# Attention blocks and MoE 1 groups in another order, some vector work on other engines

## Chip, cores and metric

One core of one Trainium2 chip runs the whole program. The metric is the device time of one execution, in microseconds; lower is better.

## The reference

Attention over 4 batches, 8 heads, 576 positions, head size 64 (heads 0 to 3 with a local mask of 32 positions, heads 4 to 7 with a mask of equal position modulo 32), and behind it two feed-forward stages on 2304 tokens of 512 columns, all in float32:

```python
scores = np.where(masks[None], scale * np.matmul(q, k.transpose(0, 1, 3, 2)), -1e9)
attn = np.exp(scores - np.max(scores, axis=-1, keepdims=True))
attn = attn / (np.sum(attn, axis=-1, keepdims=True) + 1e-09)
x = np.matmul(attn, v).transpose(0, 2, 1, 3).reshape(B * S, H * D)
h = x @ w_in                                    # 512 -> 2048
x = (h * np.tanh(softplus(h))) @ w_out          # MoE 1 (Mish), 2048 -> 512
g = x @ w_gate
y = (g / (1 + np.exp(-g)) * (x @ w_val)) @ w_out2   # MoE 2 (SwiGLU), 512 -> 1536 -> 512
```

## The kernel before

**Precision.** Each float32 operand of a big matmul is kept as a high part and a low part (what is left). A product is three matmuls of 512 columns: high by high, high by low, low by high (`mm3`, L81 to L83). `split_hi` copies to the high part, on ScalarE (L74); `split_lo` subtracts (L79), on VectorE or GpSimd. The weights come as 64-bit numbers; each weight tile of 128 x 512 is turned into float32 by four steps (`w_ops`: a at L206 and L207, b L210, c L213, d L216), each one VectorE instruction, the first with a square on ScalarE besides; step d also issues the load of a later weight (`w_load`, L138). Then `w_hi` (ScalarE) and `w_lo` split it. `w_step(n)` does n of these steps, `w_flush` the splits.

**Attention.** There are 48 units (16 pairs of heads, 3 units each; unit 3i + 2 is the last of pair i). Two units make a block; `at_pair` issues block k by the list PAIR, whose entries are a function and a lag: it works on units 2k and 2k + 1 and finishes older ones, down to unit 2k - 5. The steps of a unit: `at_qk` (scores on TensorE, L303, and mask, minimum and copy on VectorE, L315), `at_exp` (ScalarE, L330), `at_norm` (1e-9 added on VectorE, L343, reciprocal on VectorE, L344, multiply on GpSimd, L345), `at_tr` (transposes on TensorE, L360), `at_copy` (VectorE, L374), `at_pv` (TensorE, L387), `at_hi` (ScalarE) and `at_lo` (VectorE) into `xh` and `xl`, the input of MoE 1. `at_load` and `at_v` issue the transfers of q, k and v on SP's queue. Blocks 0 to 23 start units; 24 to 26 only finish.

**MoE 1.** The work is in stages n = 0 to 19: n = 5q + c is column chunk q of the hidden layer and token chunk c. A stage's first half is 16 groups (`g1_step`: hidden tile f, input tile kc, one `mm3` each); after kc = 3 the result h is copied out by VectorE (`act_a` with keep, L489). Then `act_m` does the four Mish on ScalarE, with a table load ahead of and behind them (L495, L496), `act_c` splits the results into `g`, and the second half is 16 more groups (`g2_by_e`). Input tile kc of tokens 0 to 511 needs the low parts of unit 3kc + 2 of the first batch; the next chunk needs units 12 to 23.

**The order** is written out by hand; each engine runs its queue in that order. First ten dummy matmuls (`spin`, L733) and the first loads. Then a loop of 15 steps k: block k; dummies by KEEP (6 in steps 1 to 5); `w_flush` and WSTEPS[k] weight steps; up to two groups of FIRST, each with a due time; and entries of the list `todo` (Mish, splits of g). With 15 blocks done the rest of stages n = 1 and 2 and the second halves of n = 0 and 1 follow, 58 groups from the point where block 15 starts; behind each group `fill` is called, every fifth of which starts a block. From n = 3 on there is no attention left.

## Time and profile before

| | us |
|---|---|
| median of 3 runs (lowest, highest) | 918.61 (917.64, 918.65) |
| the profiled execution | 920.39 |
| its span | 918.60 |
| TensorE busy | 900.7 (98%) |
| VectorE busy | 597.4 (65%) |
| ScalarE busy | 384.3 (42%) |
| GpSimd busy | 157.2 (17%) |

PE is TensorE, PEld its weight loads, DVE is VectorE, ACT is ScalarE, POOL is GpSimd, SPq the queue that issues transfers. A row of the timeline is one instruction, or several alike (xcount), with its start, its duration, and in brackets the idle time ahead of it and what ended that. Matmuls overlap, so prices are read from start to start. PEclk is the granted clock of TensorE, 1.00 being full speed.

### The profile page before, as it was taken

To read this page: it belongs to the slowest core of one execution; us is meant where nothing else is said; L and a number is where in the kernel's file an instruction comes from. 1 tells how busy PE (TensorE), PEld (TensorE's weight loads), DVE (VectorE), ACT (ScalarE), POOL (GpSimd) and SP (SyncE) were. 2 spreads that over 40 slices of the span, in tenths; PEclk is the share of its full clock that TensorE was granted. 3 is DMA by queue.
4 is the path that set the end of the run, shared out by engine and by line. 5 is a ranking of instruction groups with operands and counts; after the bars stand their busy time and mean duration, and the time that the engine had idled before them with its cause. 6 is when DMAs were issued, how large, how long until landed. Compare 5 with 4: busy or idle time off the path is not lost.

```text
span 918.6 us, 13867 instructions
## 1 busy us (share of the span) xinstructions
PE 900.7 (98%) x4984; PEld 754.8 (82%) x4984; DVE 597.4 (65%) x1382; ACT 384.3 (42%) x951; POOL 157.2 (17%) x153
## 2 busy tenths in 40 slices
PE   8988999999999999999999999999999999999998
PEld 5776877888888888888889888888888888888886
DVE  4896656768977797769556788848435644334434
ACT  4767765525443444435233553423324423322230
POOL 1333331400000000000022322203113221112211
PEclk8979999999999999999999999999999999999999
DMA  7876431324653255424106888675532545552322
GB/s 266 297 242 213 144 100 39 131 93 150 213 180 121 92 184 185 165 85 161 70 1 250 302 328 303 260 286 189 189 118 112 207 152 192 185 204 86 144 92 92
DMA packets 48499, 156.70 MB, mean 171 GB/s; under 512 B 5296, under 2 KB 11824, under 8 KB 48432
## 3 DMA queue, kind: packets, MB, share of 16 engines
q1 hardware_dynamic: 48432, 155.83, 47.7%
q8 instruction: 39, 0.64, 0.3%
q14 instruction: 28, 0.23, 0.1%
HBM read 119.64 MB, written 36.18 MB: 170 GB/s over the span
## 4 chain that ended last, share of the span: by engine, by line
PE 93%; DVE 2%; ACT 1%; POOL 1%; DMA 1%; issue 1%; SPq 0%; ACTq 0%; POOLq 0%; DVEq 0%
PE y L83 21%; PE h L83 21%; PE o L83 16%; PE cXv L83 7%; PE cXg L83 7%; PE c L83 4%; PE cZv L83 4%; PE cZg L83 4%; PE sc L303 2%; PE xp L387 2%; PE cYv L83 2%; PE cYg L83 2%; PE tp L360 1%; PE wp L733 1%; DMA qk<-in_qk_dram 1%; ACT pt L330 1%
## 5 line engine op out<-in xcount | busy, mean ns | idle before, releaser
L83 PE MATMUL y<-g,w 128*128 128x512 f32 (+1 forms) x960 | 202.0, 369 | 0.0
L83 PEld LDWEIGHTS y<-g,w 128*128 128x128 f32 x960 | 167.0, 189 | 29.9
L83 PE MATMUL h<-xh,w 128*128 128x512 f32 (+1 forms) x640 | 190.9, 375 | 0.0
L83 PE MATMUL o<-wr,fs 128*128 128x512 f32 x648 | 149.6, 389 | 0.0
L83 PEld LDWEIGHTS o<-wr,fs 128*128 128x128 f32 x648 | 121.3, 188 | 25.0
L83 PEld LDWEIGHTS h<-xh,w 128*128 128x128 f32 x640 | 117.9, 191 | 20.4
L83 PE MATMUL h<-xl,w 128*128 128x512 f32 (+1 forms) x320 | 119.0, 372 | 0.0
L491 ACT ACTIVATE u<-h 128x512 f32<-128x512 f32 (+1 forms) x68 | 37.2, 547 | 140.7 <-PE h L83 140.7
L79 POOL TENSOR_TENSOR fs<-k,fs 128x512 fp32r<-128x512 f32 x36 | 48.5, 1346 | 267.5 <-ACT fs L74 206.4
L720 DVE TENSOR_TENSOR acc<-acc,o 128x512 f32<-128x512 f32 x90 | 61.3, 685 | 48.5 <-PE o L83 48.5
L330 ACT ACTIVATE pt<-pt,sm 108x64 f32<-108x64 f32 (+1 forms) x160 | 55.8, 351 | 35.2 <-DVE sm L315 34.0
L83 PEld LDWEIGHTS h<-xl,w 128*128 128x128 f32 x320 | 61.2, 191 | 9.7
L79 POOL TENSOR_TENSOR B<-acc,B 128x512 fp32r<-128x512 f32 x6 | 8.4, 1395 | 297.6 <-ACT B L74 297.6
L74 ACT CAST fs<-k 128x512 fp32r<-128x512 f32 x36 | 22.4, 622 | 87.9 <-DVE k L675 37.6
L83 PE MATMUL cXv<-T,wr 128*128 128x512 f32 x216 | 55.0, 390 | 0.0
L83 PE MATMUL cXg<-T,wr 128*128 128x512 f32 x216 | 54.9, 389 | 0.0
L661 DVE TENSOR_TENSOR k<-cZg,k 128x512 f32<-128x512 f32 x12 | 8.3, 692 | 71.1 <-PE cZg L83 71.1
L79 DVE TENSOR_TENSOR g<-u,g 128x512 fp32r<-128x512 f32 (+1 forms) x68 | 43.1, 654 | 13.9 <-ACT g L74 13.9
L74 ACT CAST ws<-wt 128x512 fp32r<-128x512 f32 x60 | 37.0, 616 | 36.0 <-DVE wt L216 29.1
L74 ACT CAST g<-u 128x512 fp32r<-128x512 f32 (+1 forms) x80 | 44.6, 574 | 15.8 <-PE y L83 15.7
L83 PEld LDWEIGHTS cXv<-T,wr 128*128 128x128 f32 x216 | 40.5, 188 | 8.7 <-ACT k L658 0.3
L83 PEld LDWEIGHTS cXg<-T,wr 128*128 128x128 f32 x216 | 40.5, 188 | 8.6 <-DVE k L661 0.2
(102 smaller groups left out, 1419.7 us busy)
## 6 DMA issues: line engine op xcount, KB each, us to landing
raw<-in_w_dram SPq DMA_DIRECT2D x54, 512.0 KB, 3.8
qk<-in_qk_dram SPq DMA_DIRECT2D x16, 898.0 KB, 6.7
wr<-wd_g_S SPq DMA_DIRECT2D x24, 512.0 KB, 6.7
wr<-wd_v_S SPq DMA_DIRECT2D x24, 512.0 KB, 7.4
wr<-wd_p SPq DMA_DIRECT2D x24, 512.0 KB, 4.6
wr<-wd_g_W SPq DMA_DIRECT2D x18, 512.0 KB, 6.3
wr<-wd_v_W SPq DMA_DIRECT2D x18, 512.0 KB, 7.1
rawl<-in_w_dram SPq DMA_DIRECT2D x14, 512.0 KB, 5.8
```

The source lines that it names most:

```text
L74: nc.scalar.copy(hi, src)
L79: eng.tensor_tensor(out=lo, in0=src, in1=hi.bitcast(F32), op=ALU.subtract)
L83: nc.tensor.matmul(o, lhsT=lhs, rhs=rhs, start=first and i == 0, stop=last and i == 2, skip_group_check=more)
L303: nc.tensor.matmul(sc[:2 * nq, jj * w:(jj + 1) * w], lhsT=t[:, 2 * j * nq:2 * (j + 1) * nq], rhs=t[:, QW + j0:QW + j0 + nk], start=True, s ...
L330: nc.scalar.activation(out=pt[:, jj], in_=pt[:, jj], func=AF.Exp, scale=-1.0, bias=sm[:, 0, jj:jj + 1], accum_out=sm[:, 1, jj:jj + 1],)
L360: nc.tensor.transpose(tp[:k, o:o + n], src, ident[:n, :n])
L387: nc.tensor.matmul(xp[64 * h:64 * h + 64, o:o + nq - skip], lhsT=vt[:nk, jj, 64 * h:64 * h + 64], rhs=ts[:nk, c0 + h * nq + skip:c0 + (h + ...
L491: nc.scalar.activation(out=u, in_=p, func=AF.Mish)
L661: nc.vector.tensor_tensor(out=t, in0=p, in1=t, op=ALU.add)
L720: nc.vector.tensor_tensor(out=acc[c][:, t], in0=acc[c][:, t], in1=o, op=ALU.add)
L733: nc.tensor.matmul(wp, lhsT=wz[:, :128], rhs=wz, start=True, stop=True)
```

## The change

- The 15 steps take the groups of each step from a table, GROUPS: 28 groups in steps 4 to 14 instead of 19. In four steps DOS says how many entries of `todo` are done.
- 22 of the 32 early weight steps stay in the 15 steps, and earlier; ten go to the first ten fills. The low parts of weights are made on GpSimd in the middle of a block (`at_w`), or on VectorE in a fill; low parts of g of n = 0 to 2 are made on VectorE.
- The fills start blocks at twelve places of a table, PAIR_AT. There are 52 fills. The second half of n = 0 runs by three banks at a time (`g2_by_3`).
- 1e-9 is added on GpSimd, in a step of its own (`at_add`).
- Dummies: 6, 6, 6, 5, 3, 3 in steps 1 to 6.
- The first transfer of q and k is cut in three (k, then q of three tiles, then six); the second one and the first weight are issued ahead of the first three loads of v.

```diff
-KEEP = {k: 6 for k in range(1, 6)}
+KEEP = {1: 6, 2: 6, 3: 6, 4: 5, 5: 3, 6: 3}
-ND = 15
-FILLS = 5
-FIRST = (
-    (0, 0, 9), (0, 1, 10), (1, 0, 13), (1, 1, 14), (0, 2, 15), (1, 2, 16), (0, 3, 17), (1, 3, 18),
-    (2, 0, 19), (2, 1, 20), (2, 2, 21), (2, 3, 22), (3, 0, 22), (3, 1, 22), (3, 2, 22), (3, 3, 22),
-)
-WSTEPS = (0, 2, 2, 2, 2, 2, 2, 2, 3, 3, 3, 3, 3, 3, 0)
+GROUPS = {
+    4: ((0, 0, 0),),
+    5: ((0, 0, 1), (0, 1, 0)),
+    6: ((0, 1, 1), (0, 0, 2)),
+    7: ((0, 1, 2), (0, 2, 0), (0, 2, 1)),
+    8: ((0, 0, 3), (0, 1, 3), (0, 2, 2)),
+    9: ((0, 2, 3), (0, 3, 0), (0, 3, 1)),
+    10: ((0, 3, 2), (0, 3, 3)),
+    11: ((1, 0, 0), (1, 1, 0), (1, 2, 0), (1, 0, 1), (1, 1, 1)),
+    12: ((1, 2, 1), (1, 0, 2)),
+    13: ((1, 1, 2), (1, 2, 2)),
+    14: ((1, 0, 3), (1, 1, 3), (1, 2, 3)),
+}
+WSTEPS = (0, 2, 3, 3, 3, 3, 2, 2, 1, 1, 1, 1, 0, 0, 0)
+WFILL = 10
+DOS = {11: 1, 12: 3, 13: 3, 14: 2}
+PAIR_AT = (0, 3, 10, 14, 17, 20, 24, 28, 32, 43, 47, 51)
...
     def w_step(n):
         for _ in range(n):
             if not wq:
-                w_flush(1)
                 wq.extend(w_ops())
...
-    def load_qk(i):
+    def load_qk(i, cuts=((0, QW + KW),)):
...
-        nc.sync.dma_start(t, qk[4 * b + hp])
+        for c0, c1 in cuts:
+            nc.sync.dma_start(t[:, c0:c1], qk[4 * b + hp, :, c0:c1])
...
+    def at_add(u):
+        pt, sm = st[u]
+        r = sm[:, 1, :pt.shape[1]]
+        nc.gpsimd.tensor_scalar_add(r, r, 1e-9)
+
     def at_norm(u):
...
-        nc.vector.tensor_scalar_add(r, r, 1e-9)
         nc.vector.reciprocal(r, r)
...
+    def at_w(u):
+        w_lo(nc.gpsimd)
+
     PAIR = [
         (at_norm, -2),
+        (at_add, -1),
...
         (at_norm, -1),
+        (at_w, -1),
         (at_lo, -5),
...
         (at_copy, -2),
+        (at_add, 0),
     ]
...
-        eng = nc.gpsimd if n < 3 else nc.vector
-        todo.insert(1, lambda: split_lo(eng, g[:, 1, :nt], u, g[:, 0, :nt]))
+        todo.insert(1, lambda: split_lo(nc.vector, g[:, 1, :nt], u, g[:, 0, :nt]))
...
+    def g2_by_3(n, fill, free):
+        nt = CHUNKS[n % NCH][1]
+
+        def bank():
+            return ps.tile([128, 512], F32, tag="mm", name="y", bufs=3)[:, :nt]
+
+        y = [bank() for _ in range(3)]
+        for f in range(QF):
+            for e in range(3):
+                g2_mm(n, y[e], e, f)
+                fill()
+                if f == QF - 1:
+                    y_out(n, y[e], e)
+        y.append(bank())
+        for f in range(QF):
+            g2_mm(n, y[3], 3, f)
+            free(f)
+            fill()
+        y_out(n, y[3], 3)
...
-        load_qk(0)
+        n = 6 * LB
+        load_qk(0, ((QW, QW + KW), (0, n), (n, 3 * n)))
         nc.sync.dma_start(cst, consts)
+        load_qk(1)
+        w_load()
         for u in range(3):
             load_v(u)
-        load_qk(1)
-        w_load()
         load_qk(2)
...
-        steps = [(0, f, kc, t) for f, kc, t in FIRST]
-        steps += [(n, f, kc, (20, 23, 26, 29)[kc]) for n in (1, 2) for f in range(QF) for kc in range(4)]
-        for k in range(ND):
+        for k in range(len(WSTEPS)):
             at_pair()
             spin(KEEP.get(k, 0))
-            w_flush()
+            w_hi()
             w_step(WSTEPS[k])
-            for _ in range(2):
-                if steps[0][3] <= 2 * k + 1:
-                    g1_step(*steps.pop(0)[:3])
-                do(3 if len(todo) > 10 else 2 if len(todo) > 5 else 1)
-        w_flush()
+            for x in GROUPS.get(k, ()):
+                g1_step(*x)
+                if todo:
+                    do(DOS.get(k, 0) if x is GROUPS[k][0] else 0)
         fills = [0]
 
         def fill():
-            if fills[0] % FILLS == 0:
+            if fills[0] in PAIR_AT:
                 at_pair()
+            if fills[0] < WFILL + 2:
+                w_lo(nc.vector)
+                w_hi()
+                w_step(fills[0] < WFILL)
             fills[0] += 1
...
+        steps = [(n, f, kc) for n, fs_ in ((1, (3,)), (2, range(QF))) for f in fs_ for kc in range(4)]
...
             while steps and steps[0][0] == n:
-                g1_step(*steps.pop(0)[:3])
                 fill()
+                g1_step(*steps.pop(0))
...
                 if n == 2:
                     wfill[0] += WF
+                    w_lo(nc.vector)
+                    w_hi()
                     w_step(wfill[0] // 16)
...
-            g2_by_e(n - 1, fill2, lambda f: act_c(n, f))
+            (g2_by_3 if n == 1 else g2_by_e)(n - 1, fill2, lambda f: act_c(n, f))
```

## Rows read from the trace of the kernel before

**Rows 1.** Windows: length, busy time by engine, PEclk, DMA share, GB/s.

```profile
core 0: us, PE busy (x) PEld busy (x) DVE busy (x) ACT busy (x) POOL busy (x), PEclk, DMA share, GB/s
14.74:87.73 72.99, 65.91 (x656) 53.36 (x655) 62.21 (x327) 52.04 (x233) 24.98 (x33) 0.90 0.75 249
87.73:96.93 9.20, 6.94 (x62) 5.83 (x61) 4.25 (x26) 5.62 (x24) 5.80 (x6) 0.98 0.14 45
96.93:164.36 67.43, 65.68 (x604) 54.73 (x603) 41.93 (x224) 42.87 (x166) 20.08 (x26) 1.00 0.32 102
164.36:914.84 750.48, 750.47 (x3625) 634.36 (x3623) 483.38 (x773) 277.40 (x504) 103.92 (x83) 1.00 0.47 168
```

**Rows 2.** Waits of TensorE in the whole span: us in total, times, longest.

```profile
PE tp L360 <- POOL pt L345: 6.0, 5, 2.3
PE tp L360 <- DVE sm L315: 4.0, 3, 2.3
```

**Rows 3.** Windows of 2 us, columns as in rows 1.

```profile
56.00:58.00 2.00, 0.00 (x0) 0.00 (x0) 1.97 (x8) 0.00 (x0) 0.42 (x1) 0.86 0.88 223
58.00:60.00 2.00, 1.75 (x6) 1.46 (x7) 1.97 (x19) 1.77 (x10) 0.81 (x2) 0.50 0.95 369
```

**Rows 4.** Timeline of TensorE: starts of blocks 18 to 20, and a dense half stage.

```profile
109.42 1.15 PE L387 MATMUL xp<-ts,v 128*64 128x54 f32 x28
...
115.96 1.14 PE L387 MATMUL xp<-ts,v 128*64 128x54 f32 x32
...
122.31 0.88 PE L387 MATMUL xp<-ts,v 128*64 128x54 f32 x14
...
175.24 11.04 PE L83 MATMUL y<-g,w 128*128 128x512 f32 x48
186.12 0.28 PE L83 MATMUL h<-xh,w 128*128 128x256 f32 x1
```

**Rows 5.** Timeline of VectorE: block 10 up to its first weight instruction.

```profile
50.17 0.16 DVE L343 TENSOR_SCALAR sm<-sm 128x3 f32<-128x3 f32 x1
50.37 0.17 DVE L344 RECIPROCAL sm<-sm 128x3 f32<-128x3 f32 x1
...
53.39 0.68 DVE L210 SCALAR_TENSOR_TENSOR wtmp<-raw,wtmp 128x512 int32<-128x512 int32 x1
```

**Rows 6.** The weight steps by tile: ns min/median/max, first and last start.

```profile
L207 DVE TENSOR_SCALAR wtmp<-raw x10: 407/416/427, 12.8 to 160.0; 128x512 int32<-128x512 int32 x10
L210 DVE SCALAR_TENSOR_TENSOR wtmp<-raw,wtmp x10: 678/692/710, 13.2 to 161.6; 128x512 int32<-128x512 int32 x10
L213 DVE SCALAR_TENSOR_TENSOR wtmp<-raw,wtmp x10: 675/679/1185, 19.4 to 162.8; 128x512 int32<-128x512 int32 x10
L216 DVE SCALAR_TENSOR_TENSOR wtmp<-w,wtmp x10: 673/692/1692, 20.1 to 164.0; 128x512 f32<-128x512 f32 x10
```

**Rows 7.** Timeline of SP's queue and of TensorE at the start.

```profile
1.66 1.51 SPq L288 DMA_DIRECT2D v<-in_v_loc_dram  x3
3.21 0.43 SPq L279 DMA_DIRECT2D qk<-in_qk_dram  x1
...
10.04 1.57 PE L303 MATMUL sc<-qk 128*128 128x96 f32 x6 [1.68 <-DMA qk<-in_qk_dram]
```

**Rows 8.** Timeline of ScalarE: the Mish of n = 0, and what follows it.

```profile
80.04 1.28 ACT L495 ACT_TABLE_LOAD   x1
...
84.83 0.62 ACT L74 CAST g<-u 128x512 fp32r<-128x512 f32 x1
```

**Rows 9.** Timeline of GpSimd and VectorE: a low part and an addition beside it.

```profile
61.36 1.52 POOL L79 TENSOR_TENSOR w<-wtmp,w 128x512 fp32r<-128x512 f32 x1 [1.99 <-ACT w L74]
...
61.67 1.24 DVE L343 TENSOR_SCALAR sm<-sm 108x3 f32<-108x3 f32 x1
```

**Rows 10.** Timeline of GpSimd: two multiplies of different size.

```profile
29.98 0.51 POOL L345 TENSOR_TENSOR pt<-pt,sm 108x192 f32<-108x192 f32 x1 [2.25 <-DVE sm L344]
...
40.61 0.67 POOL L345 TENSOR_TENSOR pt<-pt,sm 128x288 f32<-128x288 f32 x1 [2.54 <-PE sc L303]
```

**Rows 11.** What ended the idle time ahead of L343: us, times.

```profile
  ACT pt L330: 0.4, 2
```

## The prediction

> **What bounds the kernel now.** I read the windows first, cut at four points of TensorE's own timeline: the start of block 2 (14.74), the start of block 15, with which the fills begin (87.73), the start of block 16 (96.93), and the first matmul of the stage that follows attention, n = 3 (164.36). From 164.36 to 914.84 TensorE is busy 750.47 of 750.48 us at a clock of 1.00 [rows 1]. Nothing of the change lies behind 164.36 but a few low parts, so whatever the change gives or takes is a shift of that point, and it goes to the end one for one. Ahead of it the stretches are not full: in 14.74 to 87.73 TensorE is busy 65.91 of 72.99 us, and its granted clock is 0.90 on the mean; VectorE is busy 62.21 us, nearly as long [rows 1].
>
> Then the waits of TensorE: they end with the normalised probabilities, written by GpSimd behind VectorE's reciprocal (6.0 us), or with VectorE (4.0 us) [rows 2]. Last the clock: TensorE had done nothing from 56 to 58 us, and from 58 on its clock was 0.50, the lower of its two levels [rows 3]. So in blocks 2 to 14 VectorE sets the pace, TensorE waits for it, and its clock falls besides.
>
> **Prices.** A group is 3 matmuls. 48 dense ones took 186.12 - 175.24 = 10.88 us, so a group is 0.68 us and a dummy matmul of the same length about 0.23. A block with five groups, where TensorE was full, took 6.54 and 6.35 us; less 5 x 0.68 that leaves 3.05 us of attention on TensorE for a block [rows 4]. On VectorE a block runs from 50.17 to the first weight instruction at 53.39 without a wait: 3.22 us, of which the addition of 1e-9 takes 0.20 (50.17 to 50.37), twice [rows 5]. Without the additions it is 2.82. A weight step takes (0.42 + 0.69 + 0.68 + 0.69) / 4 = 0.62 us of VectorE, and a copy of h about 0.69 like the others of its size [rows 6].
>
> These prices hold for the kernel before. Blocks 2 to 14 need 13 x 3.22 + 30 weight steps x 0.62 + 4 copies x 0.69 = 63.2 us of VectorE (busy: 62.21), and 13 x 3.05 + 22 groups x 0.68 + 24 dummies x 0.23 = 60.1 us of TensorE. The stretch took 72.99, so 12.9 us over TensorE's own work. The fills (58 groups, nine full blocks, and three that only finish, some 3.2 us) need 27.5 + 3.2 + 39.4 = 70.1 us and took 9.20 + 67.43 = 76.6: 6.5 over. Of these, 9.20 - 6.45 = 2.75 lie in block 15, which stands behind the first Mish and in which GpSimd is busy 5.80 us [rows 1].
>
> **The change part by part.**
>
> *Start.* The second unit of block 1 waited 1.68 us for the second q and k transfer, whose issue stood behind three loads of v (1.51 us of SP's queue) [rows 7]. Now it stands ahead of them, but behind two more pieces of the first, so it is issued about 1.51 - 2 x 0.42 = 0.7 us earlier, with the bytes of v no longer ahead of it. The gain is between 0.7 and 1.7 us; I take 1.2, the middle. The cut of the first transfer gives nothing: the ten dummies ahead of it run to about 5.5 us anyway. The loads of v now also stand behind the first weight; block 2 needs them some 3 us after the second q and k.
>
> *Blocks 2 to 14.* 28 groups instead of 22 and 23 dummies instead of 24. TensorE: 13 x 3.05 + 28 x 0.68 + 23 x 0.23 = 64.0 us. VectorE: the additions leave (26 x 0.20 = 5.2 us), and of the weight steps 20 remain here instead of 30 (6.2 us less); copies of h become 7 (2.1 more) and four low parts of g come from GpSimd (4 x 0.65). That is 13 x 2.82 + 20 x 0.62 + 7 x 0.69 + 2.6 = 56.5 us. So the bound goes from VectorE to TensorE. Block by block VectorE is longer only in blocks 2 and 3 (2.82 + 3 x 0.62 = 4.68 against 3.05 + 6 x 0.23 = 4.43), together 0.5 us. What is late next is the Mish of n = 0: two table loads and four activations hold ScalarE from 80.04 to 84.83, 4.8 us [rows 8], and now stand in block 11. Behind them in ScalarE's queue are the high parts of block 12, for which block 12's second group waits. Block 11 has five groups: 3.05 + 3.4 = 6.45 us on TensorE, and ScalarE, which has 52.04 / 13 = 4.0 us a block of its own [rows 1] and starts some 0.8 into it (an estimate), comes out of the Mish about 9.6 us behind the block's start, so block 12 waits about 1.0 us and block 14 0.6: 1.6 us. For the rest (groups that wait for low parts of their own block, weights that arrive in the block that uses them, GpSimd in VectorE's way) I keep 2.5 us of the 12.9 lost before; the bounds are 0 and, if nothing gets better, 12.9. Sum 64.0 + 0.5 + 1.6 + 2.5 = 68.6, against 72.99: 4.4 us earlier, with six groups more done.
>
> *Fills.* 52 groups: 27.5 + 3.2 + 35.4 = 66.1 us. Block 15's 2.75 us are gone with their Mish. The other 3.8 us I keep. New: ten weight steps run in the first ten fills, and the Mish of n = 1 falls between blocks 16 and 17. There ScalarE has 4.8 + 4.0 us beside 3.05 + 7 x 0.68 = 7.8 of TensorE, and the last weight's high part queues behind it: I put 2.0 us on it (bounds 0 and 4.8, the whole Mish). Sum 66.1 + 3.8 + 2.0 = 71.9 against 76.6: 4.7 us.
>
> *1e-9 on GpSimd.* Its price there isn't in the trace. From 0.51 us for 192 and 0.67 for 288 elements a partition, a GpSimd operation of 3 elements would be about 0.2 us, an estimate [rows 10]. GpSimd and VectorE hold each other up: the addition at 61.67 took 1.24 us instead of 0.16, beside a GpSimd low part from 61.36 to 62.88 [rows 9]. Turned round, an addition on GpSimd can stand behind one weight instruction of VectorE: 0.69. So the reciprocal can come between 0.0 and 0.9 us later, at no cost while the exponentials end earlier than that; VectorE waited for them 2 times in 48, 0.4 us [rows 11]. I take nothing for it, since that row is the nearest.
>
> The Trainium skill (SBUF — State Buffer, SBUF: two separate sides) says why: VectorE and GpSimd share one pair of ports, locked for a whole instruction, and VectorE wants it with two SBUF inputs or in a fast mode. The trace agrees (1.24 us against 0.16). That rule speaks against putting more small work on GpSimd, and is the last rival's.
>
> *Low parts.* Four weight low parts (the one at 61.36 took 1.52 us) [rows 9] leave GpSimd's end of a block; those that stay are queued in mid-block, behind the multiply that TensorE waits for and not ahead of the next one. Priced in the 2.5 kept.
>
> **Sum.** 1.2 + 4.4 + 4.7 = 10.3 us. The profiled execution, 920.39 us (span 918.60), becomes 910.1; the median of the runs, 1.78 us below it, becomes 918.61 - 10.3 = 908.3.
>
> **Rivals.**
>
> *The early part fills wholly.* No loss but the 0.5: blocks 2 to 14 64.5, fills 66.1, start 1.7. That is 8.5 + 10.5 + 1.7 = 20.7 us, 897.9. For it: six groups fill just what was idle and the clock need never fall. Against: the Mish still holds ScalarE three times.
>
> *The loss only moves.* TensorE runs in order; a group that waits for a low part made in its own block stops the next block's scores behind it, and the clock falls as it did at 58. If the 12.9 and 6.5 us stay, moving six groups changes no sum, and only the start and a dummy are won: 918.61 - 1.4 = 917.2. For it: blocks 5, 6, 8, 11, 12 and 14 use low parts of the same block. Against: VectorE, which those waited for, has 7 us less to do.
>
> *GpSimd takes the lead.* If the reciprocal at the head of a block waits for the addition, everything behind it on VectorE (copy, scores, low parts) waits too: 0.9 us for each of 22 full blocks is 19.8 us, against the 10.3, so 928. It decides from the point where the exponentials of a block's first unit end less than 0.9 us before VectorE reaches the next block. Before, they hardly ever did [rows 11]; but VectorE now runs ahead, and ScalarE is late behind each Mish.
>
> **How the numbers follow.** Forecast (903 to 914) 0.55; wholly filled 0.17; loss moves 0.16; GpSimd leads 0.12. Both last ones lie above 917 and the full rival mostly below 900, so 900 to 917.5 leaves out about 0.2. A measurement can tell about 0.2%, 1.8 us, from no change: faster (under 916.8) is the first two and a third of the third, 0.77; same is the rest of it, 0.11; slower 0.12.
>
> **What would show it.** Right: stage n = 3 starts near 154 us and is dense from there; block 15 starts near 82 with 28 groups done; the wait of 1.68 us is gone or halved; VectorE's busy share of blocks 2 to 14 falls below TensorE's; no stretch of clock 0.50 behind the first blocks, or one at block 12. Wrong: TensorE waiting for GpSimd longer than 10 us in all (last rival); low parts of the same block as the main releaser and a clock of 0.50 (the third); any gap behind 164.36, which would put the change's effect where I have looked for none.

## The result: 0.85% shorter, and where the time went

| | before | changed |
|---|---|---|
| median of 4 runs each (lowest to highest), us | 918.52 (917.64 to 918.65) | 910.83 (908.95 to 911.47) |
| the profiled execution (its span) | 920.39 (918.60) | 911.30 (909.5) |

The ratio of changed to before is 0.9915, with a 95% interval of 0.9898 to 0.9932. The medians are 7.7 us apart, the two profiled executions 9.1; the forecast was 10.3.

The windows of the changed kernel, cut at the same points of TensorE's timeline as [rows 1] (start of block 2, of block 15, of block 16, of block 17, of block 18, first matmul of n = 3):

```profile
core 0: us, PE busy (x) PEld busy (x) DVE busy (x) ACT busy (x) POOL busy (x), PEclk, DMA share, GB/s
13.50:81.30 67.80, 64.40 (x673) 52.19 (x677) 53.29 (x296) 51.47 (x233) 32.33 (x57) 1.00 0.75 250
81.30:87.06 5.76, 5.42 (x57) 4.54 (x56) 5.62 (x27) 3.37 (x18) 1.79 (x4) 1.00 0.53 183
87.06:98.52 11.46, 9.16 (x68) 6.81 (x67) 8.28 (x30) 10.07 (x28) 3.27 (x5) 1.00 0.65 214
98.52:105.82 7.30, 6.10 (x60) 4.56 (x59) 5.29 (x27) 3.66 (x18) 1.56 (x4) 1.00 0.70 241
105.82:155.20 49.38, 47.48 (x460) 39.55 (x459) 33.08 (x165) 31.15 (x126) 11.57 (x27) 1.00 0.27 87
155.20:905.60 750.40, 750.40 (x3630) 634.48 (x3626) 483.18 (x778) 277.65 (x504) 98.21 (x79) 1.00 0.47 168
```

The last cut stands 0.08 us ahead of the first matmul of n = 3 (155.28), from which the table below counts.

A count has to be set right first. The text ahead of the prediction gives the fills of the kernel before 58 groups, the prediction gives its blocks 2 to 14 22. By its loop, 19 groups stand in the 15 steps and one more is issued ahead of block 15, so blocks 2 to 14 hold 20 and the fills 60. The trace has the 60 matmuls of 20 groups (column PE, matmuls of L83 alone):

```profile
14.74:87.73 72.99, 20.05 (x60) 12.79 (x60) 0.90 0.75 249
```

The changed kernel holds 28 and 52, so eight groups were moved and not six.

Three things are to be seen beside [rows 1]. From n = 3 on nothing changed: 750.40 us against 750.48, without a gap. Blocks 2 to 14 took 67.80 us instead of 72.99 with eight groups more; VectorE's busy time there fell from 62.21 to 53.29 and now lies well below TensorE's 64.40; the clock is 1.00. And a new hole is open in blocks 16 and 17, where TensorE is busy 9.16 + 6.10 of 11.46 + 7.30 us.

The waits of TensorE in blocks 2 to 14 (us in total, times, longest):

```profile
PE h L93 <- POOL w L89: 1.5, 3, 0.7
PE xp L401 <- DVE wtmp L217: 0.4, 1, 0.4
PE h L93 <- ACT xh L84: 0.4, 1, 0.4
PE tp L374 <- DVE sm L325: 0.4, 1, 0.4
PE tp L374 <- POOL pt L359: 0.4, 1, 0.4
```

The wait for normalised probabilities of [rows 2] (now L359), 6.0 us in the whole span and 5.1 of them here, is down to 0.4. What leads now is groups that wait for low parts of a weight (L89).

### The profile page after: what moved, and what is told of

The parts are those of the page before. It is cut to its first block, busy times and chain, and to the rows that moved or that the text cites. A ratio compares the mean times of both kernels' runs of the same rounds, so it can differ in the third digit from the quotient of the medians.

```text
span 909.5 us, 13847 instructions
## 1 busy us (share of the span) xinstructions
PE 894.2 (98%) x4978; PEld 748.7 (82%) x4983; DVE 593.7 (65%) x1349; ACT 383.7 (42%) x951; POOL 151.6 (17%) x186
## 4 chain that ended last, share of the span: by engine, by line
PE 93%; ACT 3%; DVE 2%; POOL 1%; DMA 1%; issue 0%; SPq 0%; ACTq 0%; POOLq 0%; DVEq 0%
PE h L93 21%; PE y L93 21%; PE o L93 16%; PE cXg L93 7%; PE cXv L93 7%; PE c L93 4%; PE cZv L93 4%; PE cZg L93 4%; PE sc L313 2%; PE xp L401 2%; PE cYv L93 2%; PE cYg L93 2%; ACT pt L340 1%; PE tp L374 1%; DMA cst<-in_consts_dram 1%; DVE pt L325 1%
## 5 line engine op out<-in xcount | busy, mean ns | idle before, releaser
L93 PE MATMUL h<-xh,w 128*128 128x512 f32 (+1 forms) x640 | 189.0, 372 | 1.9 <-POOL w L89 1.5
L89 POOL TENSOR_TENSOR fs<-k,fs 128x512 fp32r<-128x512 f32 x36 | 48.7, 1352 | 267.1 <-ACT fs L84 208.5
L89 DVE TENSOR_TENSOR g<-u,g 128x512 fp32r<-128x512 f32 (+1 forms) x80 | 51.0, 658 | 16.2 <-ACT g L84 16.2
L84 ACT CAST fs<-k 128x512 fp32r<-128x512 f32 x36 | 22.4, 622 | 88.1 <-DVE k L714 37.5
L89 POOL TENSOR_TENSOR B<-acc,B 128x512 fp32r<-128x512 f32 x6 | 8.4, 1394 | 299.9 <-ACT B L84 299.9
L84 ACT CAST ws<-wt 128x512 fp32r<-128x512 f32 x60 | 37.0, 616 | 35.6 <-DVE wt L226 31.7
L84 ACT CAST g<-u 128x512 fp32r<-128x512 f32 (+1 forms) x80 | 44.3, 574 | 15.5 <-PE y L93 15.5
```

Source lines behind the costliest of these rows:

```text
L84: nc.scalar.copy(hi, src)
L89: eng.tensor_tensor(out=lo, in0=src, in1=hi.bitcast(F32), op=ALU.subtract)
L93: nc.tensor.matmul(o, lhsT=lhs, rhs=rhs, start=first and i == 0, stop=last and i == 2, skip_group_check=more)
```

## The experiments

One table carries many of the verdicts. Each row is one profiled execution; the columns are us between points of TensorE's timeline as above, the last the sum from block 2 to n = 3. With before's order (before, e2, e9, e5) block 15 has five groups and the fills 60; in the others it has three and the fills 52, and blocks 2 to 14 hold eight groups more.

| kernel | block 2 at | 2 to 14 | 15 | 16, 17 | 18 to n = 3 | sum |
|---|---|---|---|---|---|---|
| before | 14.74 | 72.99 | 9.20 | 12.49 | 54.94 | 149.62 |
| changed | 13.50 | 67.80 | 5.76 | 18.76 | 49.46 | 141.78 |
| e2_b_add_pool | 13.94 | 69.26 | 11.59 | 12.50 | 54.84 | 148.19 |
| e9_b_glo_dve | 12.58 | 70.42 | 7.68 | 12.50 | 54.14 | 144.74 |
| e5_b_add_glo | 13.67 | 69.32 | 7.79 | 12.48 | 53.73 | 143.32 |
| e7_undone | 14.32 | 72.28 | 8.94 | 14.17 | 50.05 | 145.44 |
| e1_add_dve | 12.52 | 69.25 | 5.97 | 19.37 | 49.82 | 144.41 |
| e10_glo_pool | 12.44 | 67.62 | 5.20 | 18.79 | 50.16 | 141.77 |
| e4_no_mish1 | 12.11 | 67.25 | 5.76 | 16.72 | 49.47 | 139.20 |
| e3_mish_late | 12.15 | 67.28 | 5.75 | 16.73 | 51.88 | 141.64 |
| e6_w15 | 11.49 | 69.98 | 9.11 | 13.85 | 49.44 | 142.38 |
| e8_no_dummies | 12.10 | 66.65 | 5.74 | 20.18 | 49.47 | 142.04 |
| e11_w28 | 11.59 | 70.49 | 5.75 | 14.45 | 49.46 | 140.15 |
| e12_best | 12.67 | 68.91 | 5.75 | 14.44 | 49.46 | 138.56 |

Two things limit it. Kernels with one order of transfers differ by up to 2 us in the start of block 2. And before's own row holds some us of lowered clock in blocks 2 to 14 (0.90) that most executions of that kernel have less of: in the runs beside e1, 17 executions of it took 915.57 to 921.02 us, those above 920 at a mean clock of 0.988 to 0.991, the others at 0.992 to 0.998; its profiled one has 0.988 and 920.39 us. The profiles of e2, e9, e5 and e7 lie within 0.8 us of their own medians. So stages are compared between kernels of a like clock, and the whole by the ratios, each against runs of before on the same chip.

### Which of the placements did it

**e1_add_dve.** The changed kernel with the additions of 1e-9 back on VectorE.

```diff
     def at_norm(u):
...
+        nc.vector.tensor_scalar_add(r, r, 1e-9)
         nc.vector.reciprocal(r, r)
...
-        (at_add, -1),
...
-        (at_add, 0),
```

> The changed kernel with the additions of 1e-9 back on VectorE, all else as changed. My theory (in blocks 2 to 14 TensorE now sets the pace, VectorE has room): 26 x 0.20 = 5.2 us of VectorE come back into a stretch of 67.8 us in which it was busy some 53, so little of it is seen: block 15 starts 0 to 2 us later than 81.30, the total is 0 to 2 us longer. Rival (the additions on GpSimd stand in the way of the reciprocals): block 15 starts 1 to 2 us earlier, the total is 1 to 2 us shorter.

Measured: 914.31 us against 917.06, ratio 0.9960 (0.9945 to 0.9976). From block 2 to n = 3 it is 2.6 us longer than the changed kernel, 1.45 in blocks 2 to 14 and the rest in the fills, a little more than the 0 to 2 us that I expected. Its window of blocks 2 to 14:

```profile
12.52:81.77 69.25, 65.05 (x673) 52.31 (x678) 57.28 (x324) 52.20 (x234) 22.46 (x31) 1.00 0.74 252
```

VectorE has 4.0 us more in blocks 2 to 14 (57.28 against 53.29) and still stays below TensorE, yet the stretch is longer. So in the changed order the move of the additions is worth some 2.6 us, by one profiled execution of each, and by the ratios rather more.

**e2_b_add_pool.** The kernel before, with that one move.

```diff
+    def at_add(u):
+        pt, sm = st[u]
+        r = sm[:, 1, :pt.shape[1]]
+        nc.gpsimd.tensor_scalar_add(r, r, 1e-9)
+
     def at_norm(u):
...
-        nc.vector.tensor_scalar_add(r, r, 1e-9)
         nc.vector.reciprocal(r, r)
...
     PAIR = [
         (at_norm, -2),
+        (at_add, -1),
...
         (at_copy, -2),
+        (at_add, 0),
```

> The kernel before with only the additions of 1e-9 moved to GpSimd. My theory (VectorE sets the pace of blocks 2 to 14 of the kernel before): up to 26 x 0.20 = 5.2 us off that stretch; block 15 starts 2 to 5 us before 87.73 and the total is 2 to 5 us shorter. Rival (latency between the engines sets the pace, or GpSimd gets in the way): within 1 us of before, or longer.

Measured: 918.79 us against 917.06, ratio 1.0014 (1.0002 to 1.0025): not shorter. Its windows of blocks 2 to 14 and of block 15:

```profile
13.94:83.20 69.26, 60.26 (x652) 48.67 (x655) 56.82 (x300) 50.41 (x227) 31.51 (x58) 0.99 0.80 266
83.20:94.79 11.59, 8.58 (x62) 6.88 (x61) 4.66 (x27) 6.65 (x30) 8.05 (x10) 0.85 0.14 45
```

VectorE's timeline in block 15, here and in the kernel before:

```profile
87.66 0.69 DVE L495 COPY u<-h 128x512 f32<-128x512 f32 x1 [3.82 <-POOL g L79]
```

```profile
91.16 0.69 DVE L489 COPY u<-h 128x512 f32<-128x512 f32 x1 [3.81 <-POOL g L79]
```

Block 15 gives 2.4 us away. VectorE's copy of h stands 3.82 us behind a low part of g on GpSimd, but it does so for 3.81 us in the kernel before too, so this wait is not what the move cost. The larger part is the clock. From the end of TensorE's longest wait to the end of block 15 the same matmuls took 5.50 us here (first row) and 3.91 in the kernel before (second row):

```profile
89.29:94.79 5.50, 5.50 (x18) 4.14 (x18) 2.39 (x16) 3.67 (x18) 4.67 (x6) 0.69 0.00 0
93.02:96.93 3.91, 3.91 (x18) 3.00 (x18) 2.43 (x16) 3.63 (x18) 2.64 (x3) 1.00 0.00 0
```

Blocks 2 to 14 are 3.7 us shorter, which I first put down to the 5.4 us that VectorE has less to do there. That reading fell: TensorE's waits for normalised probabilities and for VectorE's minimum in this stretch come to 6.1 and 1.8 us, against 5.1 and 1.7 in the kernel before. What went is the lowered clock of [rows 3]. TensorE waited just as long at that place (2.29 us before, 2.31 in e9, 2.10 here):

```profile
57.19 0.41 PE L364 MATMUL tp<-cst,pt 108*128 108x108 f32 x2 [2.10 <-POOL pt L349]
```

Behind it the clock stayed at 1.00 (windows of 2 us):

```profile
57.00:59.00 2.00, 1.81 (x10) 1.29 (x12) 1.77 (x17) 1.68 (x9) 1.21 (x4) 1.00 1.02 375
```

while the kernel before had 0.50 until past 66 us; the last window of 2 us that lies wholly at that level:

```profile
64.00:66.00 2.00, 2.00 (x13) 2.00 (x13) 1.05 (x12) 0.57 (x3) 0.00 (x0) 0.50 0.93 273
```

Nor did VectorE gain much by its lighter load: its reciprocal now waited for the addition on GpSimd. VectorE's waits for it in blocks 2 to 14, in e2 and in the changed kernel (us in total, times, longest):

```profile
DVE sm L348 <- POOL sm L342: 4.5, 9, 1.1
```

```profile
DVE sm L358 <- POOL sm L352: 0.5, 2, 0.3
```

That is 4.5 of the 5.4 us that VectorE saved, the mechanism of the rival in which GpSimd gets in the way. In the changed order the same additions are waited for 0.5 us. It fits that the move pays there (e1) and not here.

**e9_b_glo_dve.** The kernel before, with only the low parts of g of n = 0 to 2 on VectorE.

```diff
-        eng = nc.gpsimd if n < 3 else nc.vector
+        eng = nc.vector
```

> The kernel before with only the low parts of g of n = 0 to 2 on VectorE. With the additions moved too it was 0.9929 of before, with the additions alone 1.0014. My theory (in block 15 VectorE's copy of h waits for GpSimd's low part of g, and the clock may fall in the wait): block 15 takes 6.5 to 8 us instead of 9.20, blocks 2 to 14 stay at 72 to 74, the total is 1.5 to 4 us shorter than before. Rival (the two moves only gain together): within 1 us of before.

Measured: 914.08 us against 916.85, ratio 0.9963 (0.9945 to 0.9980). Windows of blocks 2 to 14 and of block 15:

```profile
12.58:83.00 70.42, 61.92 (x656) 49.72 (x655) 63.04 (x330) 51.83 (x232) 25.37 (x33) 0.96 0.81 270
83.00:90.68 7.68, 7.40 (x62) 6.25 (x61) 6.93 (x30) 6.08 (x27) 2.61 (x3) 0.91 0.19 58
```

Block 15 is 1.5 us shorter, GpSimd's busy time there 2.61 instead of 5.80, and VectorE's copy of h, which starts at 83.78, no longer waits for a low part. Blocks 2 to 14 have nearly the same work as before and the same wait of 2.3 us; they took 70.42 us at a mean clock of 0.96 instead of 72.99 at 0.90, since behind that wait it was lowered for some 3.5 us and not for ten:

```profile
58.00:60.00 2.00, 2.00 (x31) 1.90 (x31) 1.97 (x3) 2.00 (x8) 1.11 (x1) 0.50 0.74 278
60.00:62.00 2.00, 2.00 (x19) 1.96 (x19) 1.73 (x13) 0.56 (x4) 0.92 (x2) 0.87 0.58 135
```

So 70.42 less some 1.7 us (2.00 us at 0.78, 2.00 at 0.50, 2.00 at 0.87 in the windows from 56 to 62, each counted with what is missing to 1.00) is the least that this stretch takes without the fall (68.7 us, an estimate; less is won where TensorE would have waited anyway). e2's 69.26 lies between the two: its gain in this stretch is small, if there is one.

**e5_b_add_glo.** Both moves together on the kernel before: e2's diff and e9's.

> The kernel before with the additions of 1e-9 on GpSimd and the low parts of g of n = 0 to 2 on VectorE, nothing else. With the additions alone, blocks 2 to 14 took 69.26 us instead of 72.99, but block 15 took 11.59 instead of 9.20, with VectorE's copy of h behind the low part of g on GpSimd (3.82 us). My theory: that low part is what takes it back; without it block 15 takes 7 to 9 us and the total is 4 to 7 us shorter than before. Rival (block 15 is long by the Mish in ScalarE's queue, whoever makes the low part): block 15 stays at 10 us or more and the total within 2 us of before.

Measured: 912.90 us against 918.05, ratio 0.9929 (0.9904 to 0.9954). Window of block 15:

```profile
82.99:90.78 7.79, 6.99 (x63) 5.74 (x62) 6.09 (x30) 6.70 (x30) 3.91 (x6) 1.00 0.24 80
```

Blocks 2 to 14 are as in e2 (69.32), and VectorE waits for the additions there for the same 4.5 us. Block 15, 11.59 us there, is 7.79; from block 18 on it is 1.1 us shorter than e2. The two placements, with the order and the transfers of the kernel before, are worth 0.71%, most of the change's 0.85%. By the medians that is more than the two alone add up to (1.0014 x 0.9963 = 0.9977). But the intervals of e5 and e9 overlap, and the 1.4 us by which e5 is shorter than e9 from block 2 to n = 3 are no more than e9's lowered clock can have cost. So the gain that the profiles show is that of the low parts in block 15; that the addition adds to it in the old order is not shown.

**e10_glo_pool.** The changed kernel with the low parts of g back on GpSimd for n < 3.

```diff
-        todo.insert(1, lambda: split_lo(nc.vector, g[:, 1, :nt], u, g[:, 0, :nt]))
+        todo.insert(1, lambda: split_lo(nc.gpsimd if n < 3 else nc.vector, g[:, 1, :nt], u, g[:, 0, :nt]))
```

> The changed kernel with the low parts of g of n = 0 to 2 back on GpSimd, all else as changed. My theory: the additions then queue on GpSimd behind 1.3 us low parts in steps 12 to 14, and block 15's VectorE waits as it did before: blocks 12 to 15 take 2 to 4 us longer, the total is 2 to 5 us longer than the changed kernel. Rival (in the changed order TensorE has groups enough to cover it): within 1 us.

Measured: 911.54 us against 916.85, ratio 0.9944 (0.9927 to 0.9961). Block 2 to n = 3 takes 141.77 us, the changed kernel 141.78. The ratio lies a little above the changed kernel's, with intervals that overlap, so the two can't be told apart: my theory fell, the rival came. In the changed order these low parts are done spread over steps 12 to 14 instead of heaped on block 15, and there their engine makes no difference that shows.

**e7_undone.** Nearly the reverse of e5: the changed order, groups and dummies, with the additions on VectorE, the low parts of g on GpSimd, the transfers in before's order, and all 32 weight steps in the 15 steps.

```diff
 (e1's and e10's edits)
-WSTEPS = (0, 2, 3, 3, 3, 3, 2, 2, 1, 1, 1, 1, 0, 0, 0)
-WFILL = 10
+WSTEPS = (0, 2, 3, 3, 3, 3, 2, 2, 2, 2, 2, 2, 2, 2, 2)
+WFILL = 0
...
-        load_qk(0, ((QW, QW + KW), (0, n), (n, 3 * n)))
+        load_qk(0)
         nc.sync.dma_start(cst, consts)
+        for u in range(3):
+            load_v(u)
         load_qk(1)
         w_load()
-        for u in range(3):
-            load_v(u)
```

> The changed kernel with four of its parts undone: the additions on VectorE, the order of the first transfers as before, the low parts of g of n = 0 to 2 on GpSimd, the ten weight steps in the 15 steps. What is left of the change is the table of groups, the places of the blocks, the banks by three and the place of the weights' low parts. My theory (the groups can't use time that VectorE doesn't give): blocks 2 to 14 take 3 to 7 us longer than the changed kernel's 67.8, and the total is 3 to 8 us longer than that of the changed kernel, at or a little under that of before. Rival (the groups do it nearly alone): the total is within 2 us of the changed kernel.

Measured: 915.62 us against 918.05, ratio 0.9969 (0.9957 to 0.9981). Blocks 2 to 14:

```profile
14.32:86.60 72.28, 65.64 (x679) 52.37 (x678) 61.27 (x326) 54.00 (x237) 27.40 (x36) 1.00 0.69 233
```

Eight more groups (8 x 0.68 = 5.4 us of TensorE) went into a stretch of about the same length; in the fills they are missing and 3.5 us are won (73.16 against 76.63). TensorE's waits for VectorE's minimum and for normalised probabilities in this stretch, 1.7 and 5.1 us in the kernel before, are

```profile
PE tp L375 <- DVE sm L325: 1.8, 2, 1.2
PE tp L375 <- POOL pt L360: 1.5, 2, 0.8
```

at about the same load of VectorE (61.27 against 62.21). So the longer of the two waits went mostly with the order of the groups. The length that is left goes with VectorE's load, as the kernels of the changed order show among each other, at a clock of 1.00: with 61.27 us of VectorE 72.28, with 58.42 (e6) 69.98, with 57.28 (e1) 69.25, with 53.29 (the changed kernel) 67.80. That is 0.4 to 0.6 us of the stretch for each us of VectorE. Each of these kernels moves work of other engines too, so that VectorE alone is the cause is likely and not shown. The order alone (groups, places of the blocks, banks by three, low parts of the weights and dummies, which no run parts) is worth 0.31%, the placements alone 0.71% (e5), and the whole change 0.85%; the new transfers and the ten weight steps in the fills are in neither of the two.

### The hole in blocks 16 and 17

TensorE's own work there is 2 x 3.05 + 11 x 0.68 = 13.6 us; the stretch took 18.76. The changed kernel's timelines show the chain, first ScalarE, then VectorE, then TensorE:

```profile
91.90 1.28 ACT L515 ACT_TABLE_LOAD   x1
93.19 2.20 ACT L515 ACTIVATE u<-u 128x512 f32<-128x512 f32 x4
95.41 1.28 ACT L516 ACT_TABLE_LOAD   x1
96.70 0.62 ACT L84 CAST w<-wtmp 128x512 fp32r<-128x512 f32 x1
...
93.42 0.69 DVE L226 SCALAR_TENSOR_TENSOR wtmp<-w,wtmp 128x512 f32<-128x512 f32 x1
97.35 0.69 DVE L89 TENSOR_TENSOR w<-wtmp,w 128x512 fp32r<-128x512 f32 x1 [2.90 <-ACT w L84]
...
97.37 1.22 PE L93 MATMUL y<-g,w 128*128 128x512 f32 x3 [1.48 <-ACT w L84]
103.98 1.22 PE L93 MATMUL y<-g,w 128*128 128x512 f32 x3 [1.20 <-ACT w L84]
```

VectorE's last step of the weight ends at 94.1; its high part (L84, on ScalarE) then stands behind the Mish of n = 1, which holds ScalarE from 91.90 to 96.69; the low part on VectorE stands behind the high part, and TensorE stands behind both. At 103.98 it happens without a Mish: the weight's last step on VectorE ended at 100.16, and its high part stood behind the exponentials of block 17 in ScalarE's queue:

```profile
103.33 0.60 ACT L84 CAST w<-wtmp 128x512 fp32r<-128x512 f32 x1
```

**e4_no_mish1.** The changed kernel without the Mish of n = 1, to see what it holds up.

```diff
-            todo.append(lambda n=n: act_m(n))
+            if n == 2:
+                todo.append(lambda n=n: act_m(n))
```

> The changed kernel without the Mish of n = 1: its four activations and both table loads are left out, so a part of MoE 1 isn't computed. It gives the whole price of that Mish. My theory: blocks 16 and 17 lose 4 to 5 us and the total is 4 to 5.5 us shorter; if the run with the Mish queued later gets nearly as far, it was the place and not the work. Rival (blocks 16 and 17 are long by VectorE's seven weight steps in them): less than 2 us shorter.

Measured: 908.02 us against 917.06, ratio 0.9900 (0.9885 to 0.9914). Blocks 16 and 17 still take 16.72 us. Their window:

```profile
85.12:101.84 16.72, 14.68 (x126) 11.45 (x125) 13.66 (x56) 9.00 (x40) 4.82 (x9) 1.00 0.76 254
```

TensorE's timeline in block 16 and in block 17:

```profile
90.91 3.69 PE L93 MATMUL y<-g,w 128*128 128x512 f32 x15 [0.82 <-DVE u L509]
...
100.00 1.92 PE L93 MATMUL y<-g,w 128*128 128x512 f32 x6 [1.22 <-ACT w L84]
```

So the Mish costs 2.0 us, and 3.1 of the 5.2 are there without it: my expectation that the Mish is most of it fell. VectorE is busy 13.66 of 16.72 us. The weight's chain through VectorE, ScalarE and VectorE again still ends too late for the group that reads it (1.22 us of wait), and a copy of h (L509), queued on VectorE between two weight steps, holds TensorE 0.82 us, as it does in the changed kernel.

**e3_mish_late.** The same Mish queued at the 12th fill.

```diff
+            if fills[0] == 11:
+                todo.append(lambda: act_m(1))
             fills[0] += 1
...
-            todo.append(lambda n=n: act_m(n))
+            if n == 2:
+                todo.append(lambda n=n: act_m(n))
```

> The changed kernel with the Mish of n = 1 queued at the twelfth fill, behind the last weight's high part, and not at the fifth. My theory (the 11.46 us of block 16 and the 7.30 of block 17 are long, 3.65 and 1.5 over 7.81 and 5.77, since two weights' high parts stand behind the Mish in ScalarE's queue): TensorE's waits for these high parts (2.7 us) go, blocks 16 and 17 lose 3 to 4.5 us, and the total is 2 to 4 us shorter, 0 to 1 us being given back in blocks 18 to 20. Rival (ScalarE simply has too much work there, whatever its order): the waits move to blocks 18 to 20 and the total stays within 1 us.

Measured: 910.28 us against 917.06, ratio 0.9925 (0.9905 to 0.9944). Window of block 20:

```profile
111.96:120.98 9.02, 7.61 (x60) 6.12 (x59) 5.28 (x28) 5.18 (x28) 1.56 (x4) 0.81 0.44 158
```

Blocks 16 and 17 gain the 2.0 us of e4, and the Mish takes them back where it now stands: block 20 takes 9.02 us instead of 7.17, with a wait of 1.41 us for VectorE's minimum and a clock that falls behind it. Nothing is won from block 2 to n = 3 (141.64 against 141.78): the rival came.

**e6_w15.** All 32 weight steps in the 15 steps, none in the fills; nothing else changed.

```diff
-WSTEPS = (0, 2, 3, 3, 3, 3, 2, 2, 1, 1, 1, 1, 0, 0, 0)
-WFILL = 10
+WSTEPS = (0, 2, 3, 3, 3, 3, 2, 2, 2, 2, 2, 2, 2, 2, 2)
+WFILL = 0
```

> The changed kernel with the ten weight steps back in the 15 steps (two in each of steps 6 to 14), none in the fills. Without the Mish of n = 1 blocks 16 and 17 still took 16.72 us instead of 13.58, so their seven and more weight steps are suspected. My theory: blocks 16 and 17 take 14 to 16 us instead of 18.76, and blocks 2 to 14 take 0.5 to 2.5 us more (6.2 us of VectorE beside a busier TensorE); the total is 0 to 3 us shorter. Rival (VectorE is nearly the bound in blocks 2 to 14 still): these take 4 us or more longer and the total is longer.

Measured: 910.68 us against 918.05, ratio 0.9915 (0.9894 to 0.9937). Windows of blocks 2 to 14, of block 15, and of blocks 16 and 17:

```profile
11.49:81.47 69.98, 65.40 (x677) 52.40 (x677) 58.42 (x305) 54.18 (x238) 33.77 (x59) 1.00 0.77 262
81.47:90.58 9.11, 6.93 (x56) 5.72 (x55) 7.66 (x31) 3.98 (x19) 2.23 (x5) 0.81 0.63 203
90.58:104.43 13.85, 13.85 (x126) 11.69 (x125) 6.29 (x43) 10.93 (x39) 3.25 (x8) 1.00 0.52 160
```

TensorE's longest wait in block 15, on its timeline:

```profile
86.52 0.88 PE L374 MATMUL tp<-cst,pt 128*96 128x128 f32 x3 [2.18 <-DVE sm L325]
```

Blocks 16 and 17 are full now: 13.85 us, TensorE busy all of it, with the Mish of n = 1 still there. The 4.9 us come back as 2.2 in blocks 2 to 14 and 3.4 in block 15, where VectorE is late with the minimum and the clock falls. So the ten steps cost some 5 us at either place (4.9 and 5.5), the second time mostly in block 15, where I had looked for nothing. And where no weight stands behind it, the Mish of n = 1 costs these two blocks hardly anything (13.85 us against 13.6 of TensorE's own work).

### Attempts at more

**e8_no_dummies.** The changed kernel without the dummies of steps 4 to 6.

```diff
-KEEP = {1: 6, 2: 6, 3: 6, 4: 5, 5: 3, 6: 3}
+KEEP = {1: 6, 2: 6, 3: 6}
```

> The changed kernel without the dummies of steps 4 to 6 (11 matmuls, 2.5 us of TensorE). My theory (in these blocks TensorE waits for VectorE and GpSimd anyway: 5.0 to 6.0 us a block, against 4.9 to 5.1 of its work): within 1 us of the changed kernel, the clock stays at 1.00. Rival (TensorE is the bound there): 1.5 to 2.5 us shorter. Third case (the dummies hold the clock up): windows at 0.50 between 24 and 45 us, and 2 us or more longer.

Measured: 909.46 us against 918.05, ratio 0.9900 (0.9879 to 0.9921), not to be told from the changed kernel, as expected. Blocks 2 to 14 are 1.15 us shorter and their clock is still 1.00; blocks 16 and 17 are 1.4 longer:

```profile
84.49:104.67 20.18, 17.86 (x127) 14.25 (x126) 13.66 (x56) 13.73 (x46) 4.82 (x9) 0.83 0.65 219
98.00:100.00 2.00, 2.00 (x13) 2.00 (x13) 1.01 (x11) 0.47 (x3) 0.56 (x2) 0.50 0.78 226
```

The clock falls there behind the wait for a weight's high part that the changed kernel has too.

**e11_w28.** 28 of the weight steps in the 15 steps, four in the fills.

```diff
-WSTEPS = (0, 2, 3, 3, 3, 3, 2, 2, 1, 1, 1, 1, 0, 0, 0)
-WFILL = 10
+WSTEPS = (0, 2, 3, 3, 3, 3, 2, 2, 2, 2, 2, 2, 2, 0, 0)
+WFILL = 4
```

> The changed kernel with 28 weight steps in the 15 steps (two in each of steps 6 to 12) and four in the fills, so that the last weight's high part stands ahead of the Mish of n = 1 in ScalarE's queue. My theory (blocks 16 and 17 lose their 5 us to weight steps and that order; VectorE has room in steps 8 to 12): blocks 16 and 17 take 13.6 to 15.5 us instead of 18.76, blocks 2 to 14 take 0.5 to 2 us more, the total is 2 to 4 us shorter than the changed kernel. Rival (what the fills gain is lost in steps 8 to 15, as with all 32 there): within 1 us.

Measured: 907.88 us against 916.85, ratio 0.9905 (0.9890 to 0.9920). Block 15 stays at 5.75 us, blocks 16 and 17 fall to 14.45, and blocks 2 to 14 take 2.7 us more, above the 0.5 to 2 that I expected, part of it at the lower clock level:

```profile
72.00:74.00 2.00, 2.00 (x24) 1.90 (x21) 1.57 (x5) 1.44 (x6) 0.67 (x1) 0.50 0.67 147
```

From block 2 to n = 3 that is 1.6 us less than the changed kernel, where I expected 2 to 4; the intervals of the ratios overlap, so a gain is not shown.

**e12_best.** e11 and e8 together, and the constants issued ahead of the first q and k transfer.

```diff
 (e11's and e8's edits)
+        nc.sync.dma_start(cst, consts)
         load_qk(0, ((QW, QW + KW), (0, n), (n, 3 * n)))
-        nc.sync.dma_start(cst, consts)
```

> As the last one, and without the dummies of steps 4 to 6, and with the constants ahead of the first transfer of q and k. The dummies cost 1.1 us in blocks 2 to 14 and the clock fell only in the waits of blocks 16 and 17, which are gone here. My theory: 1 us less than the last one in blocks 2 to 14, 0.2 to 0.5 us at the start, the total 3 to 5.5 us shorter than the changed kernel (905 to 908 where before is 918.5). Rival (without the dummies the clock falls in another wait): a window at 0.50 and no gain over the last one.

Measured: 908.70 us against 916.85, ratio 0.9909 (0.9895 to 0.9924). It has the shortest stretch from block 2 to n = 3 of all (138.56 us), 3.2 us less than the changed kernel, but the ratio of the runs does not tell the two apart: no gain is shown over the changed kernel or over e11. Constants first gained nothing at the start: VectorE's first instruction still began at 7.27, there behind TensorE, which waited for q and k.

## Why the prediction held, point by point

Forecast 908.3, measured 910.83: the likeliest case came, 2.5 us short. Half of that (1.2) is in the sum: the fills gave 2.0 us less than forecast, blocks 2 to 14 0.8 more. The other half is that I carried a change of the profile over to the median one for one, while before's profile held more lowered clock than its median (1.78 us above it, the changed kernel's 0.47). That it came so near is luck in part: the lowered clock of before's profile filled up the term of blocks 2 to 14, and the wrong count of groups made the term of the fills 1.4 us smaller than my own prices give. The sum for the two profiles, term by term:

| term | forecast | measured |
|---|---|---|
| start | 1.2 | 14.74 - 13.50 = 1.2 |
| blocks 2 to 14 | 4.4 | 72.99 - 67.80 = 5.2 |
| fills | 4.7 | 76.63 - 73.98 = 2.7 |
| sum | 10.3 | 9.1 |

**Start: the size came out, the reasons were incomplete.** The five profiles with before's order of transfers start block 2 at 12.58 to 14.74, 13.85 on the mean; the eight with the changed order at 11.49 to 13.50, 12.24 on the mean. That is 1.6 us, inside the bounds of 0.7 and 1.7, but with 2 us between runs of one order, so no single pair of profiles shows it. I had overlooked that cutting the transfer moves the constants behind its pieces, on whose arrival VectorE's first instruction waits. The changed kernel's start on VectorE (6.78 us in the kernel before, there behind TensorE):

```profile
7.27 0.26 DVE L325 CUSTOM_DVE_ANT_0 pt<-sc,cst 128x96 f32<-128x96 f32 x1 [7.27 <-DMA cst<-in_consts_dram]
```

With the constants first, e12 started no earlier, since q and k are next in line.

**Blocks 2 to 14: the loads right, the mechanism only in part.** The forecast was that TensorE would take over from VectorE, with 64.0 us on TensorE and 56.5 on VectorE; the profile has 64.40 and 53.29. But the stretch still goes with VectorE's load in the changed order (e7, e6 and e1), at 0.4 to 0.6 us for each us of it, where a bound on TensorE alone would give nothing. And that VectorE set the pace of the kernel before is not borne out: there e2 took 5.4 us from VectorE, and TensorE's waits stayed. Of the 5.2 us some 2 to 3.5 are the clock of before's profile (920.39, against medians of 916.85 to 918.52 of its runs), which I had read as a cost that goes with the waits. The losses were put at 4.6 us (0.5 in blocks 2 and 3, 1.6 behind the first Mish, 2.5 kept) and were 67.80 - 64.0 = 3.8. Of the 1.6 behind the Mish, the waits show only the 0.4 for ScalarE (L84); the block behind it had more slack than I counted. Groups that wait for low parts of weights are there, as the third rival had it, but for 1.5 us in all.

**Fills: the step that failed is the 2.0 us for the Mish of n = 1 and the ten weight steps.** It cost 18.76 - 13.58 = 5.2 us, a little above the upper bound of 4.8. I had taken that bound from the Mish alone, and put the weight steps at nothing beside it because no engine's load came near the time. Beside the weight steps the Mish costs 2.0 (e4, e3), without them at most 0.3 (e6). The rest is the weights' own chain, 3.1 us without the Mish (e4): four steps on VectorE among the attention's work, a high part on ScalarE behind the exponentials, a low part on VectorE again, one weight after another, too late for its group (1.2 us of wait), and a copy of h behind such a step (0.8); e6 without those steps has 13.85 us, all of it busy. What else I kept for the fills was too much: 3.8 us forecast, 73.98 - 66.1 - 5.2 = 2.7 measured, of which 5.76 - 5.09 = 0.7 lie in block 15. That is the wrong count: the 60 groups of the fills before needed 27.5 + 3.2 + 40.8 = 71.5 us and not 70.1, so 5.1 us were lost there and not 6.5, and 2.4 without block 15's 2.75, near what was measured. (For blocks 2 to 14 the same count makes the loss before 14.2 us and not 12.9.) With it the forecast of the fills would have been 6.1 us earlier, against 2.7 measured: the two mistakes partly cancelled. Block 15's 2.75 us are gone as forecast, but for the 0.7.

**1e-9 on GpSimd: the usual cost right, the waits not nothing.** All instructions of L352 in the changed kernel (ns least, median, longest), and who waited for them; then the longest of them and VectorE beside it:

```profile
L352 POOL TENSOR_SCALAR sm<-sm x48: 221/227/1179, 8.8 to 145.1; 128x3 f32<-128x3 f32 x24, 108x4 f32<-108x4 f32 x16, 108x3 f32<-108x3 f32 x8
...
  DVE sm L358: 2.0, 5
```

```profile
54.16 1.18 POOL L352 TENSOR_SCALAR sm<-sm 108x4 f32<-108x4 f32 x1 [0.30 <-ACT pt L340]
54.57 0.68 DVE L226 SCALAR_TENSOR_TENSOR wtmp<-w,wtmp 128x512 f32<-128x512 f32 x1
```

It takes 0.227 us, estimated at 0.2, and VectorE's reciprocal waits for it 5 times in 48, 2.0 us in all. So the last rival (928) had its mechanism and not its frequency; it came nearer in the old order, where e2's reciprocals waited 4.5 us in blocks 2 to 14 alone. The longest one took 1.18 us, above the 0.9 that I allowed. The Trainium skill (SBUF — State Buffer, SBUF: two separate sides) has GpSimd and VectorE, this one in a fast mode or with two inputs from SBUF, take turns at a shared pair of ports for a whole instruction; the two rows fit it, since the addition ends at 55.34, just behind VectorE's step with two inputs (to 55.25). The rule does not say whether the move pays: by e1 it was worth 2.6 us in the changed kernel, and by e2 nothing in the kernel before.

**Low parts: mis-sized.** I priced those of g only as 2.6 us more for VectorE. On the kernel before that move alone is worth 0.37% (e9): it takes a wait of 3.8 us on VectorE out of block 15. In the changed order it is worth nothing that shows (e10).

**The other rivals.** "Fills wholly" (897.9) failed at the 5.2 us of blocks 16 and 17 and the 3.8 of blocks 2 to 14. "The loss only moves" (917.2) is what e3 and e6 did, in the small: the 2 or 5 us they won in one block came back in another. The whole change escaped it.

What stays open: how much of e1's 2.6 us is chance, with one profiled execution of each kernel (the ratios, 0.9960 and 0.9915, have intervals that do not meet, so not all of it); and what the waits of 6.8 us in blocks 2 to 14 of the kernel before hang on, since less load on VectorE (e2) and less on GpSimd in block 15 (e9) left them, while the new order alone (e7) took them down to 3.3 us at nearly the same load.

## What to carry to other kernels

Try a placement in the order in which it is to stand: the additions on GpSimd won nothing in the old order (1.0014), where VectorE waited 4.5 us for them, and some 0.45% in the new one, where it waited 0.5 us; the low parts of g won 0.37% in the old order and nothing that shows in the new. When a trace names a long wait behind a move, look for the same wait in the trace before. Price a moved chain of small steps on its links (step, high part, low part, matmul, each behind other work in its queue), not on engine load: the ten weight steps looked free by load and cost some 5 us at either place. And before a stage of one profile is used as the base of a sum, its clock is to be held against other executions: what was accident there is no gain to come.

## What the runs showed of the hardware that I had not expected

The clock did not answer the same wait in the same way. Behind the 2.1 to 2.3 us at one place of blocks 2 to 14 it was at 0.50 (1.2 GHz, the lower level) until past 66 us in the kernel before, for some 3.5 us in e9, whose work up to there is the same, and not at all in e2 and e5. In the changed kernel TensorE waited 1.48 us for a weight's high part (ahead of 97.37), and its clock stayed at 1.00; in e8 the wait ahead of the same group was 1.51 us, and from 97 to 103 the clock was 0.50. Behind waits of 1.48 (e11, at 69.65), 1.41 (e3, block 20), 2.18 (e6, block 15) and 2.89 us (e2, block 15) it fell too; behind 2.26 us in block 15 of the kernel before (ahead of 93.02) it stayed at 1.00. What tells these cases apart the runs do not show; a hole of this size has to be priced both with the fall and without it. The first transfers also scatter: eight kernels with the same transfers up to there started block 2 between 11.49 and 13.50 us, so a gain of 1 us at the start can't be read from a pair of profiles.
